# Pair sums of the second batch's input: adding transfers given out by GpSimd in place of GpSimd additions, in a Fourier transform with a feed-forward layer

## The chip, the cores and the metric

The kernel runs on one core of a Trainium2 chip. The metric is the device time of one execution in microseconds (us); three runs of the kernel before gave 1673.82, 1674.25 and 1674.61 us, so the median is 1674.25.

## The reference

```python
X = np.fft.fft(x, axis=1)                 # x: 8 x 3008 x 256, float32
X = np.fft.fft(X, axis=2)
x = X.real.astype(np.float32).reshape(24064, 256)
h = x @ w_in                              # 256 x 2048
g = np.where(h >= 1, h, np.where(h <= -1, 0.0, (h + 1) ** 2 / 4))
out = (g @ w_out).astype(np.float32)      # 2048 x 256
```

## The kernel before

**The work.** For each of the eight batches the kernel makes the transform in two stages of small matrix products (3008 = 64 x 47). Stage one (`stage1_sums`, product on L424) multiplies a folded input tile `x` by cosine and sine matrices into a PSUM bank called `s`, and ScalarE copies the bank to the tile `z` (`stage1_copies`, L458, four copies a tile). Stage two (L554) gives the tiles `pqh` and `pql`, high and low halves of a float32 number. From batch 1 on (`PLAIN = 1`) the input comes as seven tiles (`XT = 7`) that the host has laid out as four rows r of the same samples with signs of position and frequency turned; rows 0+1 and 2+3 are the *pair sums*, and their sum and difference are what stage one multiplies.

The feed-forward layer follows in *units*: 48 a batch, one for each of 16 blocks of 128 hidden features and each of three column chunks of 482 or 512 positions. `gemm1` (L599) makes two banks `uv` from `pqh`, `pql` and the halves `wh`, `wl` of w_in; VectorE makes `us` and `h` from them (L602, L605, L606), ScalarE the activation `a` (L611, L612), VectorE the gate in place in `h` (L629), ScalarE its high half `gh` (L632), and GpSimd the low half `gl` (`low_halves`, L652, two instructions, one for each of the two signs of position). `gemm2` (L728) adds three products to each of the four banks `acc`: `gh` by `woh`, `gh` by `wol`, `gl` by `woh`. Units 0 to 17 are an exception: they have no `gl`, since the native float32 product is used there.

**The first batch.** Until unit 23 the order of the work is written out by hand. START, AHEAD, AMID and STEPS are tables of steps by unit; a letter is a step, the number after it is its argument. There the weights, which are 64-bit floats, are turned into 32-bit ones by VectorE, ScalarE and GpSimd (`convert_*`, tiles `cv` and `raw`; `convert_scale` on GpSimd is L325), w_in is folded with the second transform by TensorE (`fold_w_in`, tile `wps`, L378), and the second batch's input is loaded (`L`, `load_x`, L163) and folded on GpSimd (`M`, `fold_next`): for tile 0 by two steps, for tiles 1 to 6 by four each: `fold_pair` twice (L186), `fold_sum` (L191), `fold_difference` (L197).

**What sets the order.** A scheduler puts every engine's instructions into one fixed sequence when the program is built; each engine then works through its own in order and waits at an instruction until what it needs is there. SyncE's queue gives out the transfers, also in order. Buffers are few: an `x` tile has four places (tag "xt"), and converting the weight piece 13 also uses one of them (`RAW[13]`), so that the load of x_2 into that place waits for VectorE's last step on piece 13 (L309), and the loads of x_5, x_4 and x_6 wait for stage one of x_0, x_1 and x_2. Stage one of most of these tiles uses a single bank ("fft"), which is free again when ScalarE has copied it.

Of the kernel before, what the change touches and what calls it, by code (L numbers as in the profile page):

```python
# [14 lines left out]
ALU = mybir.AluOpType  # L15
# [12 lines left out]
PLAIN = 1  # L28
# [18 lines left out]
def _constants():  # L47
# [36 lines left out]
)  # L84
AHEAD = {1: "p12 v2 G0 q11", 2: "b3", 3: "p13 d3", 5: "L1", 6: "u1 d4", 7: "e14", 8: "M R1", 11: "d6", 12: "e15 r2 a10 M e7", 14: "s4", 15: "M b10", 16: "M", 17: "u2 d10 Q2 M u3 B11", 19: "u4 s7 c15", 20: "Q4", 23: "d15", 27: "M", 29: "M", 32: "M"}
AMID = {0: "p11 b2", 1: "h E1 q12", 4: "q13", 5: "p14", 6: "q14 A9", 7: "f2 B9 a8", 8: "b9 c8", 9: "c6", 11: "M a7 f4", 12: "b7 e10", 14: "d13", 16: "O1", 17: "a15 e11 a14 f7", 18: "b11", 19: "u5 b14 O5", 20: "L5", 22: "u6", 23: "M", 24: "M", 28: "M M", 31: "M M", 32: "M"}
STEPS = {
    0: "c2 | D1",
    1: "L0 e5",
# [4 lines left out]
    6: "a12 d5",  # L94
    7: "b8 | b12 M s2 f3",
    8: "s3 d8 | a6 b6 e13",
    9: "r1 | c9 M",
    10: "u0 | d9 M L2",
    11: "f5 A13 R2",
    12: "s5 | c12 l11 B13 b13",  # L100
    13: "c13 d12 |",
    14: "f6 c7 d7",
    15: "M s6 Q0 |",
    16: "A11 c10 M |",
    17: "R3 | M",
    18: "O3 r3 c11 d11 M b15",
    19: "c14 d14",
    20: "L4 |",
    22: "L6 |",
    23: "u7",  # L110
    24: "M O6 | O7",
    25: "M |",
    26: "M |",
}
# [28 lines left out]
def fft_ffn_kernel(ctx: ExitStack, tc: tile.TileContext, x, xn, cst, w_in, w_out, out):  # L143
    nc = tc.nc
# [6 lines left out]
    xt, yt, zt, nyb, pq = {}, {}, {}, {}, {}  # L151
# [5 lines left out]
    def load_x(b, q):  # L157
        tag = "xt" if b or q < 4 else "gl"
        bufs = BUFS["xt"] if b or q < 4 else 4
        t = sb.tile([P, 2, CH], F32, tag=tag, name=f"x_{b}_{q}", bufs=bufs)  # L160
        if b >= PLAIN:
            t = t.rearrange("p (r u) n -> p (r u n)", u=1).rearrange("p (r n) -> p r n", r=4)[:, :, : CH // (2 if q else 4)]
            nc.sync.dma_start(t, xn[b - PLAIN, q, :, :, : t.shape[2]])  # L163
        else:
            nc.sync.dma_start(t, x[b, q])
        xt[b, q] = t

    def fold_x(b, q, engine=None):

        t = xt.pop((b, q))  # L170
        engine = engine or nc.gpsimd
        y = sb.tile([96, CH], F32, tag="y", name=f"y_{b}_{q}", bufs=1) if q == 0 else t[:96, 0]
        first = engine.tensor_tensor(y, t[:96, 0], t[:96, 1], op=ALU.add)
        yt[b, q] = y
        if q == 0:
            n = P if b else NA
            y = t[:96, 1, :n]
            ins = engine.tensor_tensor(y, t[:96, 0, :n], t[:96, 1, :n], op=ALU.subtract).ins
            tc.add_manual_dep(ins, first.ins.name, no_sync, reason="order of issue")
            yt[b, "d"] = y  # L180
        return first.ins

    def fold_pair(b, q, r):

        t = xt[b, q][: NT * NH]
        return nc.gpsimd.tensor_tensor(t[:, r], t[:, r], t[:, r + 1], op=ALU.add).ins  # L186

    def fold_sum(b, q):

        t = xt[b, q][: NT * NH]  # L190
        return nc.gpsimd.tensor_tensor(t[:, 1], t[:, 0], t[:, 2], op=ALU.add).ins  # L191
# [153 lines left out]
    def behind_vector(ins):  # L345
        last = [ins for ins in traced if ins.engine == mybir.EngineType.DVE][-1]
        tc.add_manual_dep(ins, last.name, data_sync, reason="beside VectorE's next steps")
# [130 lines left out]
    def fold_behind_activation(b, q):  # L478
        if q == 0:
            folding.extend([(b, q, fold_first_pairs), (b, q, fold_first_signs)])  # L480
            return
        folding.extend([(b, q, fold_pair, 0), (b, q, fold_pair, 2), (b, q, fold_sum), (b, q, fold_difference)])
# [6 lines left out]
    folding, ahead = [], []  # L489
    for q in range(XT):  # L490
        if q == 0:
            ahead += [(1, q, fold_first_pairs), (1, q, fold_first_signs)]
        else:
            ahead += [(1, q, fold_pair, 0), (1, q, fold_pair, 2), (1, q, fold_sum), (1, q, fold_difference)]

    def fold_next():
        if not ahead:
# [89 lines left out]
    def signs(i):  # L587
        return (slice(0, 1), slice(1, 2)) if i == n_units - 1 else (slice(0, 2),)

    def gemm1(i):  # L590
# [11 lines left out]
        nc.vector.scalar_tensor_tensor(us, nyb[b, k][:, :n], delta[:, f : f + 1], uv[0], op0=ALU.mult, op1=ALU.add)  # L602
        run_steps(AHEAD.get(i, ""))
        h = sb.tile([P, 2, CH], F32, tag="h", name=f"h_{i}", bufs=4)[:, :, :n]
# [3 lines left out]

        run_steps(AMID.get(i, ""))
        for sg in signs(i):  # L610
# [148 lines left out]
    def piece_sums(n):  # L759
# [10 lines left out]
        "m": lambda n: nc.sync.dma_start(cm, cst[:, _OFF[2] : _OFF[6]]),  # L770
        "h": lambda n: load_halves(),
        "x": lambda n: load_x(0, n),
        "y": lambda n: fold_x(0, n, nc.vector),
        "L": lambda n: load_x(1, n),
        "Y": lambda n: behind_vector(fold_x(1, n)),
        "g": lambda n: fold_x(0, n),
        "p": piece_sums,
# [29 lines left out]
    def run_steps(names):  # L807
        for s in names.split():
            steps[s[0]](int(s[1:] or 0))
# [17 lines left out]
    for i in range(n_units + LAG):  # L827
        if i < n_units:
            b, r = divmod(i, per)
            r0 = NEXT if b == 0 else 0  # L830
            if r == r0:
                pending = fft_pieces(b + 1) if b + 1 < NB else []
            if b + 2 < NB and r == LOADED[b + 2 >= PAIRED]:
                for q in range(4):
                    load_x(b + 2, q)
            gemm1(i)
            if b == 0 and units[i][2] == NFT - 2:
                load_parts(units[i][1])
# [117 lines left out]
```

## Time and profile before

| | us |
|---|---|
| median of three runs | 1674.25 |
| the profiled execution's own time | 1674.61 |
| its span, first to last instruction | 1672.4 |
| TensorE busy | 1667.3 |
| VectorE busy | 1393.8 |
| ScalarE busy | 1328.9 |
| GpSimd busy | 1189.6 |

The span is 2.2 us shorter than that execution's own time. An engine's busy time is the time in which at least one of its instructions ran. In the rows below, PE is TensorE, DVE VectorE, ACT ScalarE, POOL GpSimd, SPq the queue of SyncE. A name such as `cv` stands for all buffers of that name; L325 is line 325 of the kernel.

### The profile page before, as it was taken

How to read it: one execution, taken by the hardware profiler on the slowest of the kernel's cores; microseconds unless marked ns; L12 is line 12 of the kernel's file. 1: busy time of each engine (PE TensorE's matmuls, PEld its weight loads, DVE VectorE, ACT ScalarE, POOL GpSimd, SP SyncE). 2: the span in 40 equal slices, each digit the busy share in tenths (PEclk: the TensorE clock that was granted, in tenths of full speed). 3: DMA queues.
4: the chain of work that ended last, by engine and by line, in shares of the span. 5: the costliest groups of instructions: out<-in, count | busy, mean ns of one | idle time of the engine just before them, and what ended most of it. 6: DMA issues, size and time to landing. Idle time of an engine off the chain costs nothing.

```text
span 1672.4 us, 21444 instructions
## 1 busy us (share of the span) xinstructions
PE 1667.3 (100%) x7733; PEld 1384.9 (83%) x7733; DVE 1393.8 (83%) x1745; ACT 1328.9 (79%) x1529; POOL 1189.6 (71%) x960
## 2 busy tenths in 40 slices
PE   9999999999999999999999999999999999999999
PEld 6558888888888888888888888888888888888887
DVE  8999899878888887888878788787887877788777
ACT  6778878877888778887787877878778888777786
POOL 2458878767787677877779677796777855666664
PEclk9999999999999999999999999999999999999999
DMA  9113111110012000120010200201001010000000
GB/s 351 49 51 123 52 51 64 43 39 33 25 45 74 7 26 29 42 75 7 26 67 4 75 7 26 69 12 64 14 19 63 1 37 32 1 26 23 2 25 26
DMA packets 35705, 75.49 MB, mean 45 GB/s; under 512 B 4624, under 2 KB 13840, under 8 KB 35600
## 3 DMA queue, kind: packets, MB, share of 16 engines
q1 hardware_dynamic: 35420, 74.00, 12.4%
q8 instruction: 60, 0.98, 0.2%
q14 instruction: 45, 0.37, 0.1%
q10 hardware_dynamic: 180, 0.14, 0.0%
HBM read 46.31 MB, written 27.81 MB: 44 GB/s over the span
## 4 chain that ended last, share of the span: by engine, by line
PE 99%; DVE 1%; issue 0%; POOL 0%; DVEq 0%; POOLq 0%
PE acc L728 62%; PE uv L599 30%; PE s L424 2%; PE s L554 2%; PE wps L378 1%; PE warm_bank L752 0%; PE s L429 0%; PE acc L678 0%; DVE us L602 0%; DVE h L605 0%; DVE h L606 0%; PE ny L528 0%; DVE g L625 0%; DVE pql L243 0%; PE delta L357 0%
## 5 line engine op out<-in xcount | busy, mean ns | idle before, releaser
L652 POOL TENSOR_TENSOR gl<-h,gh 128x512 fp32r<-128x512 f32 (+1 forms) x728 | 917.7, 1283 | 383.1 <-PE acc L728 186.3
L611 ACT ACTIVATE a<-h,biases 128x1024 f32<-128x1024 f32 (+1 forms) x385 | 436.3, 1134 | 218.7 <-DVE h L606 216.5
L728 PE MATMUL acc<-gh,woh 128*128 128x512 f32 (+1 forms) x1456 | 563.1, 387 | 0.0
L728 PE MATMUL acc<-gh,wol 128*128 128x512 f32 (+1 forms) x1456 | 558.0, 383 | 0.0
L728 PE MATMUL acc<-gl,woh 128*128 128x512 f32 (+1 forms) x1456 | 557.8, 383 | 0.0
L629 DVE SCALAR_TENSOR_TENSOR h<-a,h 128x1024 f32<-128x1024 f32 (+2 forms) x367 | 522.5, 1424 | 2.0 <-ACT a L612 1.1
L602 DVE SCALAR_TENSOR_TENSOR us<-nyb,delta,uv 128x512 f32<-128x512 f32 (+1 forms) x384 | 282.6, 736 | 205.3 <-PE uv L599 203.3
L632 ACT ACTIVATE gh<-h 128x1024 fp32r<-128x1024 f32 (+2 forms) x367 | 382.8, 1043 | 83.0 <-DVE h L629 62.7
L612 ACT ACTIVATE a<-a 128x1024 f32<-128x1024 f32 (+1 forms) x385 | 395.2, 1027 | 1.0
L728 PEld LDWEIGHTS acc<-gl,woh 128*128 128x128 f32 x1456 | 272.7, 187 | 51.6
L728 PEld LDWEIGHTS acc<-gh,woh 128*128 128x128 f32 x1456 | 272.9, 187 | 49.4
L728 PEld LDWEIGHTS acc<-gh,wol 128*128 128x128 f32 x1456 | 272.8, 187 | 49.0
L605 DVE TENSOR_TENSOR h<-us,uv 128x512 f32<-128x512 f32 (+1 forms) x384 | 260.1, 677 | 52.6 <-POOL gl L652 2.1
L599 PE MATMUL uv<-pqh,wh 128*128 128x512 f32 (+1 forms) x768 | 302.4, 394 | 0.0
L599 PE MATMUL uv<-pql,wh 128*128 128x512 f32 (+1 forms) x768 | 294.3, 383 | 0.0
L599 PE MATMUL uv<-pqh,wl 128*128 128x512 f32 (+1 forms) x768 | 294.2, 383 | 0.0
L606 DVE TENSOR_TENSOR h<-us,uv 128x512 f32<-128x512 f32 (+1 forms) x384 | 257.4, 670 | 0.0
L599 PEld LDWEIGHTS uv<-pqh,wh 128*128 128x128 f32 x768 | 143.9, 187 | 30.8 <-issue 3.8
L599 PEld LDWEIGHTS uv<-pqh,wl 128*128 128x128 f32 x768 | 143.8, 187 | 30.6 <-issue 4.5
L599 PEld LDWEIGHTS uv<-pql,wh 128*128 128x128 f32 x768 | 143.8, 187 | 27.5 <-DVE pql L243 0.4
L186 POOL TENSOR_TENSOR x<-x 120x256 f32<-120x256 f32 x84 | 99.2, 1182 | 14.7 <-DVE h L629 5.3
L458 ACT ACTIVATE z<-s 64x240 f32<-64x240 f32 (+1 forms) x196 | 69.0, 352 | 4.4 <-PE s L424 1.8
(100 smaller groups left out, 786.4 us busy)
## 6 DMA issues: line engine op xcount, KB each, us to landing
x<-in_xn_dram SPq DMA_DIRECT2D x42, 512.0 KB, 3.7
out_dram<-o SPq DMA_DIRECT2D x26, 512.0 KB, 2.8
out_dram<-o SPq DMA_DIRECT2D x14, 482.0 KB, 2.8
nyb<-nyr SPq DMA_DIRECT2D x24, 256.0 KB, 3.2
x<-in_x_dram SPq DMA_DIRECT2D x8, 512.0 KB, 7.1
raw<-in_moe_w_in_dram SPq DMA_DIRECT2D x4, 512.0 KB
raw<-in_moe_w_out_dram SPq DMA_DIRECT2D x4, 512.0 KB, 8.9
part<-o SPq DMA_DIRECT2D x4, 512.0 KB
```

The source lines that it names most:

```text
L186: return nc.gpsimd.tensor_tensor(t[:, r], t[:, r], t[:, r + 1], op=ALU.add).ins
L458: nc.scalar.activation(z[to, :, at : at + n], src[:, :, t0 : t0 + n], AF.Copy)
L599: nc.tensor.matmul(t[:, :n], w[m][:, cols], r[:, m], start=(j == 0), stop=(j == 2))
L602: nc.vector.scalar_tensor_tensor(us, nyb[b, k][:, :n], delta[:, f : f + 1], uv[0], op0=ALU.mult, op1=ALU.add)
L605: nc.vector.tensor_tensor(h[:, 0], us, uv[1], op=ALU.subtract)
L606: last_h = nc.vector.tensor_tensor(h[:, 1], us, uv[1], op=ALU.add).ins
L611: nc.scalar.activation(a[:, sg], h[:, sg], AF.Relu, bias=half, scale=0.5)
L612: nc.scalar.activation(a[:, sg], a[:, sg], AF.Square)
L629: g = nc.vector.scalar_tensor_tensor(h[:, sg], a[:, sg], 1.0, h[:, sg], op0=ALU.min, op1=ALU.max).ins
L632: nc.scalar.activation(gh[:, sg], h[:, sg], AF.Copy)
L652: ins = nc.gpsimd.tensor_tensor(gl[:, sg], h[:, sg], gh[:, sg].bitcast(F32), op=ALU.subtract).ins
L728: nc.tensor.matmul(acc[:, :n], w, g[:, sg], start=(begin and j == 0), stop=(last and j == len(terms) - 1))
```

## The change

Rows 1 and 3 of tiles 1 to 6 of batch 1 are no longer loaded by SyncE. SyncE loads rows 0 and 2 alone (256 KB in place of 512 KB), and GpSimd gives out a second transfer, the step `K`, that reads rows 1 and 3 from HBM and adds them to the tile in SBUF. The twelve additions L186 of these tiles go, with the twelve steps `M` that placed them; `fold_sum` and `fold_difference` stay. Tile 0, and all later batches, are as before. K1 stands at unit 7, K3 at 8, K2 at 12, K4 at 22, K5 at 23, K6 at 24; the load L1 is at unit 5, L3 at 4, L2 at 10, L4 and L5 at 20, L6 at 22.

```diff
-    9: "r1 | c9 M",
+    9: "r1 | c9",
...
-            nc.sync.dma_start(t, xn[b - PLAIN, q, :, :, : t.shape[2]])
+            src = xn[b - PLAIN, q, :, :, : t.shape[2]]
+            if b == 1 and q:
+                nc.sync.dma_start(t[:, 0::2], src[:, 0::2])
+            else:
+                nc.sync.dma_start(t, src)
...
+    def add_pairs(q):
+
+        t = xt[1, q]
+        nc.gpsimd.dma_start(t[:, 0::2], xn[1 - PLAIN, q, :, 1::2, : t.shape[2]], accum_op=ALU.add)
...
-            ahead += [(1, q, fold_pair, 0), (1, q, fold_pair, 2), (1, q, fold_sum), (1, q, fold_difference)]
+            ahead += [(1, q, fold_sum), (1, q, fold_difference)]
...
+        "K": add_pairs,
```

Up to unit 24 TensorE, VectorE and ScalarE have the same sequence as before. Three places of the new program follow. In them `x_1_2` is tile 2 of batch 1, and the last number of a name only counts. Ten lines were added, so the changed kernel's L195 is the new transfer, L334 is the former L325, L661 the former L652, L200 and L206 the former L191 and L197, L433 the former L424, L608 and L737 the former L599 and L728.

**GpSimd around unit 12.** Before:

```order
L197 TENSOR_TENSOR x_1_1_458<-x_1_1_458 120x256
L325 TENSOR_TENSOR cv_12_522<-cv_12_522 128x512
L325 TENSOR_TENSOR cv_13_702<-cv_13_702 128x512
L316 TENSOR_TENSOR cv_7_687<-cv_7_687,raw_wol_153 128x512
L325 TENSOR_TENSOR wo_1_680<-cv_7_687 128x512
L186 TENSOR_TENSOR x_1_2_668<-x_1_2_668 120x256 x2
```

After:

```order
L206 TENSOR_TENSOR x_1_1_458<-x_1_1_458 120x256
L195 DMA x_1_2_668<-in_xn_dram 128x2x256
L334 TENSOR_TENSOR cv_12_522<-cv_12_522 128x512
L334 TENSOR_TENSOR cv_13_702<-cv_13_702 128x512
L325 TENSOR_TENSOR cv_7_687<-cv_7_687,raw_wol_153 128x512
L334 TENSOR_TENSOR wo_1_680<-cv_7_687 128x512
```

The two additions of x_1_2 stood behind the scaling of the weight pieces 12 and 13; the transfer that takes their place stands ahead of it.

**GpSimd from unit 20 on, after the change** (before, `gl_20` followed on `gl_19` at once, and the pair additions of tiles 4 to 6 stood behind `gl_23`, `gl_24`, `gl_25` and `gl_28`):

```order
L661 TENSOR_TENSOR gl_19_1043<-h_19_968,gh_19_1008 128x482 x2
L195 DMA x_1_4_1011<-in_xn_dram 128x2x256
L661 TENSOR_TENSOR gl_20_1085<-h_20_1000,gh_20_1036 128x482 x2
L334 TENSOR_TENSOR wo_3_987<-cv_15_898 128x512
L206 TENSOR_TENSOR x_1_3_445<-x_1_3_445 120x256
L195 DMA x_1_5_1004<-in_xn_dram 128x2x256
L661 TENSOR_TENSOR gl_21_1123<-h_21_1030,gh_21_1068 128x482 x2
L195 DMA x_1_6_1071<-in_xn_dram 128x2x256
L661 TENSOR_TENSOR gl_22_1158<-h_22_1057,gh_22_1107 128x482 x2
L200 TENSOR_TENSOR x_1_4_1011<-x_1_4_1011 120x256
```

The transfers of tiles 4, 5 and 6 now stand ahead of `gl_20`, `gl_21` and `gl_22`.

**TensorE at the same place, after the change** (before, each unit's `gl` products stood among its `gh` products, and the products of x_1_1, x_1_2 and x_1_3 were apart by a whole unit or two):

```order
L433 MATMUL s1_1_1_1193<-halves_340,x_1_1_458 128x120 x4
L608 MATMUL uv_26_0_1217<-pqh_0_1_297,wh0_68 128x512
L608 MATMUL uv_26_0_1217<-pqh_0_1_297,wl0_70 128x512
L608 MATMUL uv_26_0_1217<-pql_0_1_298,wh0_68 128x512
L433 MATMUL s1_1_2_1237<-halves_340,x_1_2_668 128x120 x4
L433 MATMUL s1_1_3_1321<-halves_340,x_1_3_445 128x120 x2
L737 MATMUL acc_12_0_870<-gl_20_1085,woh_498 128x482
L737 MATMUL acc_12_2_872<-gl_20_1085,woh_498 128x482
L737 MATMUL acc_12_1_871<-gl_20_1085,woh_498 128x482
L737 MATMUL acc_12_3_873<-gl_20_1085,woh_498 128x482
```

Ahead of these rows now stand the products of x_1_0 (two), the eight `gh` products of unit 20 and the six of `uv_25`; behind them come seven `gh` products of unit 21, its `gl` products in the same split manner, the other three of `uv_26`, and unit 22. The scheduler has moved the four `gl_20` products behind the stage-one products of three tiles.

## Rows read from the trace of the kernel before

**Rows 1.** The page: engines' busy time, and the chain that ended last.

```profile
PE 1667.3 (100%) x7733; PEld 1384.9 (83%) x7733; DVE 1393.8 (83%) x1745; ACT 1328.9 (79%) x1529; POOL 1189.6 (71%) x960
...
PE 99%; DVE 1%; issue 0%; POOL 0%; DVEq 0%; POOLq 0%
```

**Rows 2.** TensorE's waits for others, whole span: us in total, times, longest.

```profile
PE warm_bank L752 <- POOL warm L747: 1.3, 1, 1.3
```

**Rows 3.** Stretches: length, busy us (instructions) of each engine, clock, DMA share, GB/s.

```profile
0.00:40.00 40.00, 38.52 (x186) 26.28 (x187) 32.28 (x63) 24.27 (x47) 10.10 (x11) 1.00 0.96 363
40.00:140.00 100.00, 100.00 (x326) 60.14 (x325) 97.44 (x142) 77.66 (x102) 52.67 (x48) 1.00 0.13 48
140.00:180.00 40.00, 40.00 (x200) 34.14 (x199) 36.76 (x41) 35.85 (x50) 38.06 (x31) 1.00 0.41 138
180.00:1660.00 1480.00, 1480.00 (x6985) 1257.15 (x6984) 1221.11 (x1493) 1188.89 (x1330) 1087.72 (x872) 1.00 0.10 34
```

**Rows 4.** L186 among tile x's instructions, first 260 us: ns min/median/max, first and last start.

```profile
L186 POOL TENSOR_TENSOR x<-x x18: 726/742/1727, 72.9 to 256.7; 120x256 f32<-120x256 f32 x18
```

**Rows 5.** The same view: SyncE's issues of the loads of x from batch 1 on.

```profile
L163 SPq DMA_DIRECT2D x<-in_xn_dram x13: 327/338/1055, 31.1 to 259.5; - x13
```

**Rows 6.** Order of time, SyncE, 88 to 95 us (start, length), and its queue's waits, 60 to 100 us.

```profile
90.76 0.33 SPq L163 DMA_DIRECT2D x<-in_xn_dram  x1
91.19 2.41 SPq L367 DMA_DIRECT2D delta<-row  x4
...
SPq L163 <- DVE cv L309: 10.7, 1, 10.7
```

**Rows 7.** DMA issues, 137 to 160 us: KB each, median us from issue to landing.

```profile
x<-in_xn_dram SPq DMA_DIRECT2D x1, 256.0 KB, 3.0
```

**Rows 8.** Order of time, GpSimd, 81 to 97 us.

```profile
82.12 0.73 POOL L197 TENSOR_TENSOR x<-x 120x256 f32<-120x256 f32 x1 [3.16 <-DVE cv L281]
86.25 1.40 POOL L325 TENSOR_TENSOR cv<-cv 128x512 f32<-128x512 f32 x1 [3.39 <-DVE cv L309]
90.88 1.27 POOL L325 TENSOR_TENSOR cv<-cv 128x512 f32<-128x512 f32 x1 [3.23 <-DVE cv L309]
```

**Rows 9.** Order of time, TensorE, 89 to 97 us.

```profile
92.70 1.88 PE L378 MATMUL wps<-cv,cm 128*128 128x512 f32 x4
94.02 0.79 PE L599 MATMUL uv<-pqh,wh 128*128 128x482 f32 x1
```

**Rows 10.** Order of time, TensorE, 118 to 205 us.

```profile
137.09 0.60 PE L424 MATMUL s<-halves,x 120*128 120x120 f32 x4
137.45 0.46 PE L728 MATMUL acc<-gh,woh 128*128 128x482 f32 x1
...
140.11 0.39 PE L599 MATMUL uv<-pqh,wh 128*128 128x512 f32 x1
...
141.47 1.05 PE L424 MATMUL s<-halves,x 120*128 120x120 f32 x8
142.28 0.46 PE L728 MATMUL acc<-gh,woh 128*128 128x482 f32 x1
```

**Rows 11.** SyncE's load into the place of x_1, tile x, 142 to 143 us.

```profile
L163 SPq DMA_DIRECT2D x<-in_xn_dram x1: 339/339/339, 142.6 to 142.6; - x1
```

**Rows 12.** Groups by shape, ScalarE, 120 to 190 us: busy us, mean ns, idle before.

```profile
L458 ACT ACTIVATE z<-s 64x240 f32<-64x240 f32 x24 | 8.9, 371 | 0.4
```

**Rows 13.** Order of time, GpSimd, 0 to 330 us.

```profile
130.16 2.42 POOL L652 TENSOR_TENSOR gl<-h,gh 128x482 fp32r<-128x482 f32 x2 [1.16 <-DVE h L629]
133.77 2.72 POOL L652 TENSOR_TENSOR gl<-h,gh 128x482 fp32r<-128x482 f32 x2 [1.19 <-DVE h L629]
136.43 2.23 POOL L325 TENSOR_TENSOR wo<-cv 128x512 f32<-128x512 f32 x1
138.63 0.74 POOL L197 TENSOR_TENSOR x<-x 120x256 f32<-120x256 f32 x1
139.32 3.32 POOL L652 TENSOR_TENSOR gl<-h,gh 128x482 fp32r<-128x482 f32 x2
```

More of the change, by code (lines that the diff above doesn't have):

```diff
@@ L84 @@
 )
-AHEAD = {1: "p12 v2 G0 q11", 2: "b3", 3: "p13 d3", 5: "L1", 6: "u1 d4", 7: "e14", 8: "M R1", 11: "d6", 12: "e15 r2 a10 M e7", 14: "s4", 15: "M b10", 16: "M", 17: "u2 d10 Q2 M u3 B11", 19: "u4 s7 c15", 20: "Q4", 23: "d15", 27: "M", 29: "M", 32: "M"}
-AMID = {0: "p11 b2", 1: "h E1 q12", 4: "q13", 5: "p14", 6: "q14 A9", 7: "f2 B9 a8", 8: "b9 c8", 9: "c6", 11: "M a7 f4", 12: "b7 e10", 14: "d13", 16: "O1", 17: "a15 e11 a14 f7", 18: "b11", 19: "u5 b14 O5", 20: "L5", 22: "u6", 23: "M", 24: "M", 28: "M M", 31: "M M", 32: "M"}
+AHEAD = {1: "p12 v2 G0 q11", 2: "b3", 3: "p13 d3", 5: "L1", 6: "u1 d4", 7: "e14 K1", 8: "M R1", 11: "d6", 12: "e15 r2 a10 M e7 K2", 14: "s4", 15: "b10", 16: "M", 17: "u2 d10 Q2 u3 B11", 19: "u4 s7 c15", 20: "Q4", 22: "K4", 23: "d15", 24: "K6", 29: "M", 32: "M"}
+AMID = {0: "p11 b2", 1: "h E1 q12", 4: "q13", 5: "p14", 6: "q14 A9", 7: "f2 B9 a8", 8: "b9 c8 K3", 9: "c6", 11: "M a7 f4", 12: "b7 e10", 14: "d13", 16: "O1", 17: "a15 e11 a14 f7", 18: "b11", 19: "u5 b14 O5", 20: "L5", 22: "u6", 23: "M K5", 28: "M", 32: "M"}
 STEPS = {
@@ L96 @@
     8: "s3 d8 | a6 b6 e13",
-    9: "r1 | c9 M",
-    10: "u0 | d9 M L2",
+    9: "r1 | c9",
+    10: "u0 | d9 L2",
     11: "f5 A13 R2",
@@ L102 @@
     14: "f6 c7 d7",
-    15: "M s6 Q0 |",
+    15: "s6 Q0 |",
     16: "A11 c10 M |",
-    17: "R3 | M",
+    17: "R3 |",
     18: "O3 r3 c11 d11 M b15",
@@ L110 @@
     23: "u7",
-    24: "M O6 | O7",
+    24: "O6 | O7",
     25: "M |",
```

## The prediction

> **What bounds the kernel now.** I read the page's first part, then its chain of waits: TensorE is busy 1667.3 of 1672.4 us, and 99% of the chain that ended last is TensorE [rows 1]. Next, who it waits for: in the whole span one wait of 1.3 us, for the zeros of the warm-up at the start [rows 2]. The stretches say the same for each stage: from 40 to 1660 us TensorE is busy in every microsecond, at a granted clock of 1.00 (2.4 GHz), while GpSimd is busy 53 of 100 us from 40 to 140 and 38 of 40 from 140 to 180 [rows 3]. So nothing that makes GpSimd lighter can be seen in the time: there is no wait for it to take away, and TensorE's own products stay the same ones. What the change can do is make TensorE wait, and every wait past 40 us is lost for good, since TensorE has no idle time later to give back. The question is therefore whether the six new transfers, at their places in GpSimd's sequence, hold up something TensorE needs.
>
> **What goes.** Twelve additions L186 of 0.73 to 1.73 us [rows 4], 9 to 21 us of GpSimd. Worth nothing by the rows above. The bytes from HBM are the same, and SyncE gives out as many transfers as before.
>
> **What comes: the price of giving out a transfer.** The trace has no transfer that GpSimd gives out. Call d the time for which one holds GpSimd, from the moment its wait is over. The nearest rows are SyncE's issues of these same loads: 0.33 us as a rule, 1.06 at the longest [rows 5]. No row says that GpSimd is quicker at it than SyncE, and an adding transfer has more to do than a load, so I take 1.06, the slow end, and keep 0.33 as the low bound. For the high bound I take a GpSimd instruction that is held up beside VectorE: the same addition takes 0.73 or 1.73 us [rows 4], so add 1.0: d = 2.06. In both cases the transfer itself lands beside other work, if the sum that reads it comes late enough: K1 and K3 are given out whole units ahead of their sums, while GpSimd is half idle [rows 3], and cost nothing; the sum of x_2 stands behind four weight steps of about 1.3 us and a fifth; the sum of x_4 comes 11 us behind K4, and those of x_5 and x_6 later still. If landing took twice the 3.0 us of a 256 KB load [rows 7], that cover would still do.
>
> **What moves, place A: K2.** It needs the load of x_2 landed. SyncE gives out that load at 90.76 only, after 10.7 us of waiting for VectorE's last step on weight piece 13, whose buffer it takes [rows 6]; that does not change. A 256 KB load lands 3.0 us after its issue [rows 7]: 93.76. Before, GpSimd scaled piece 12 at 86.25 and piece 13 at 90.88 [rows 8], and TensorE used them in the two `wps` products from 92.70 on [rows 9]. Now both scalings stand behind K2: 93.76 + 1.06 (d) + 1.40 = 96.22 for piece 12, + 1.27 = 97.49 for piece 13 (durations from [rows 8]). TensorE reaches `wps` at 92.70 as before and waits 3.52; the first product takes half of 1.88 us [rows 9], to 97.16, and the second waits 0.33. **A = 3.85 us**, and d comes into it once. Everything later is shifted by it; below I go on in the times of the trace of before.
>
> **Place B: K4, K5, K6, and TensorE's new order.** Prices: twelve `acc` products from 137.45 to 140.11, so 0.222 each; six `uv` products 1.36; the products of one stage-one tile 0.81 [rows 10]; ScalarE's four copies of its bank 4 x 0.371 = 1.48 [rows 12]; one `gl` instruction 1.21, half of 2.42 [rows 13].
>
> Step 1, the bank. TensorE passes the products of x_0 at 137.45, does eight `gh` products (to 139.22) and six `uv` (140.58), then x_1 (141.39) and three `uv` (142.07). x_2 needs the bank that ScalarE copies until 141.39 + 1.48 = 142.87: a wait of 0.80. Done at 143.68; x_3 needs the next copies, until 145.16: 1.48 more. Its two products end at 145.57. Before, a whole unit of products lay between these tiles and hid the copies.
>
> Step 2, `gl_20`. The load of x_4 takes the place of x_1; before, it was given out at 142.6 [rows 11], 1.13 after x_1's products began at 141.47 [rows 10]. Now these begin at 140.58, so the load goes out at 141.71 and lands at 144.71. K4 waits for it, and `gl_20` stands behind K4: 144.71 + 1.06 = 145.77, then 1.21 twice: 146.98 and 148.19. TensorE waits from 145.57 to 146.98 (1.41), does two products, and waits 0.77 for the second half. (Before, `gl_20` began at 133.77 [rows 13], 3.7 us ahead of unit 20's first `acc` product.)
>
> Step 3, `gl_21`. GpSimd goes on with the scaling of piece 15 (1.27), the difference of x_3 (0.74 [rows 13]), K5 (1.06) and `gl_21`: 152.47 and 153.68. TensorE, from 148.63, has seven `gh` products, to 150.18: it waits 2.29, then 0.77.
>
> Step 4, `gl_22`. K6 to 154.74, halves at 155.95 and 157.16. TensorE waits 0.47 and 0.54. From there the sums of x_4 and x_5 stand between the next `gl`, at 0.73 to 0.74 each, where four instructions stood before, and I count no more.
>
> **B = 0.80 + 1.48 + 1.41 + 0.77 + 2.29 + 0.77 + 0.47 + 0.54 = 8.5 us**; d comes in three times. VectorE stands still here too, since each `h` takes the buffer that a `gl` four units before has to have read; that is the same delay, not another.
>
> **The sum.** 3.85 + 8.5 = 12.4 us with GpSimd at its short durations. At those that the same instructions had in the trace of before (2.23 for the scaling, 2.72 and 3.32 for `gl_20` and `gl_21` [rows 13]) it is 0.96 + 0.30 + 0.90 = 2.2 more, 14.6. VectorE, beside which they were long, now stands still for part of the stretch, so I take the middle, 13.5. The profiled execution took 1674.61 us: 1688.1. Against the median, 0.36 lower, 1687.8. **Forecast: 1688 us**, 0.8% slower. A measurement of this kernel tells some 0.2%, 3.3 us, from no change. With d = 0.33 and the short durations the sum is 12.4 - 4 x 0.73 = 9.5 (1684); with d = 2.06 and the long ones 14.6 + 4.0 = 18.6 (1693).
>
> **Rivals.**
>
> *The queue is not held (not slower).* If a transfer's wait were kept beside GpSimd's sequence, so that what stands behind K2 and K4 runs on, A and the waits for `gl` vanish; only the bank waits of step 1 stay: 2.3 us, 1676.9, within 0.2%. It decides at K2: the scaling of piece 12 would start near 86 and not after 94. For it: no row shows GpSimd waiting for a transfer to be given out. Against it: SyncE's queue does wait in order; the transfers of `delta` stand behind the load of x_2 and go out right after it, at 91.19 [rows 6]. The Trainium skill (DMA: Bandwidth & Descriptors, Anatomy of one DMA — SWDGE (gpsimd) path) says that DMA engines never wait on semaphores and that any such wait happens on the issuing sequencer; by that rule this rival falls, and SyncE's rows agree, while no run so far shows it for GpSimd. Chance 0.07.
>
> *Each issue is held beside VectorE (slower still).* If VectorE, busy 97 of 100 us up to 140 [rows 3], keeps GpSimd from its part in the transfer as it holds the additions, d is 2.06: 1693, up to 1697 where more instructions of place B are held by 1.0 each. For it: 0.73 against 1.73 in [rows 4]. Against: VectorE itself stands still in most of B. Chance 0.22. The Trainium skill (SBUF — State Buffer, A bandwidth-pool intuition that's wrong (but worth ruling out)) has a transfer of GpSimd at about 0.62 us alone and 3.1 beside a VectorE copy, which waits for its descriptors; if all four deciding issues were held by those 2.5 us, the estimate by that page would be 14.6 + 10 = 24.6 us, 1699; no run here shows such a transfer yet.
>
> *Less of it.* The loads of x_2 and x_4, half as large, land a microsecond earlier, and d is small: 6 to 8 us, 1681 to 1683. Chance 0.03.
>
> *A gain.* It would need TensorE to have lost time to GpSimd without a wait on record; [rows 2, 3] leave no room. Chance 0.03, a microsecond or a few.
>
> **How the numbers follow.** The forecast has 0.65, between 1684 and 1692; the held issue 0.22, the lesser loss 0.03, no change 0.07, a gain 0.03. Slower by over 0.2%: 0.65 + 0.22 + 0.03 = 0.90; within: 0.07; faster: 0.03. The range 1681 to 1697 takes in the bounds of d and both lengths of GpSimd's work, and leaves out the cases without change and the tail beyond 1697.
>
> **What the profile after would show.** TensorE's busy time about as before, the span longer. In its waits: `wps` for GpSimd's scaling, near 4 us at about 93; stage one (L433) for ScalarE's copies, about 2.3; `acc` for `gl`, about 6, all before 165 us. GpSimd idle from 83 to about 94, released by the load of x_2, and again ahead of K4. After 180 us every unit as long as before. Wrong would be: GpSimd scaling piece 12 before 93 (the queue is not held); waits of TensorE for x_5 or x_6 (adding transfers land slowly); a loss spread over the span and not in these two places.

## The result, and the profile after

The changed kernel took 1694.3 us (median of four runs, 1694.06 to 1694.79) against 1674.05 for the kernel before on the same chips (1673.82 to 1674.61): a ratio of 1.012, 95% interval 1.0108 to 1.0133, so 20.2 us slower. The forecast was 1688, the range 1681 to 1697.

The page of the changed kernel, its span, the engines' busy time and the chain that ended last, which answer to [rows 1]:

```profile
span 1692.3 us, 21449 instructions
...
PE 1675.4 (99%) x7733; PEld 1386.6 (82%) x7733; DVE 1395.2 (82%) x1745; ACT 1329.0 (79%) x1529; POOL 1180.7 (70%) x954
...
PE 94%; DVE 3%; POOL 1%; issue 1%; DMA 0%; SPq 0%; DVEq 0%; POOLq 0%
```

GpSimd is lighter by 8.9 us and six instructions, and the span is 19.9 us longer. Two things are to be seen in TensorE's figures. Its time without work is now 1692.3 - 1675.4 = 16.9 us, before it was 1672.4 - 1667.3 = 5.1: **11.8 us of new idle time**. And the same 7733 products are busy for 1675.4 us instead of 1667.3: **8.1 us in which TensorE works, but more slowly**. The prediction spoke only of the first.

TensorE's waits for others over the whole span (answering to [rows 2]; us in total, times, longest):

```profile
PE wps L387 <- POOL cv L334: 4.5, 1, 4.5
PE acc L737 <- POOL gl L661: 4.3, 7, 1.1
PE s L433 <- ACT z L467: 2.5, 2, 1.6
PE warm_bank L761 <- POOL warm L756: 1.3, 1, 1.3
```

The three new lines are the three that were forecast, and add up to 11.3 us. The stretches (length, busy us and instructions of PE, PEld, DVE, ACT and POOL, granted clock, DMA share, GB/s; answering to [rows 3]) say where:

```profile
40.00:90.00 50.00, 50.00 (x156) 28.32 (x155) 49.00 (x76) 39.40 (x53) 19.52 (x19) 1.00 0.18 52
90.00:100.00 10.00, 5.49 (x12) 2.10 (x10) 5.11 (x8) 3.09 (x3) 5.25 (x5) 0.74 0.44 105
100.00:140.00 40.00, 40.00 (x129) 24.43 (x128) 36.95 (x51) 29.99 (x38) 21.13 (x17) 0.98 0.07 27
140.00:180.00 40.00, 33.48 (x144) 25.62 (x143) 27.70 (x31) 23.89 (x37) 22.75 (x20) 0.91 0.43 117
180.00:1680.00 1500.00, 1499.67 (x7078) 1273.08 (x7077) 1238.23 (x1512) 1206.35 (x1352) 1101.97 (x884) 1.00 0.10 34
```

TensorE is idle for 4.5 us between 90 and 100, for 6.5 between 140 and 180, and for the 0.3 of a last wait at 185 us: the places A and B. In these two stretches, and at the start of the one between them (0.98), the granted clock is no longer 1.00.

GpSimd in order of time, at place A (81 to 103 us) and at place B (135 to 175 us; start, length, engine, instruction, in brackets the idle time before and what ended it):

```profile
94.67 1.12 POOL L195 DMA_DIRECT2D x<-in_xn_dram  x1 [11.48 <-DMA x<-in_xn_dram]
95.51 2.79 POOL L334 TENSOR_TENSOR cv<-cv 128x512 f32<-128x512 f32 x2
...
152.09 1.15 POOL L195 DMA_DIRECT2D x<-in_xn_dram  x1 [13.29 <-DMA x<-in_xn_dram]
152.95 2.71 POOL L661 TENSOR_TENSOR gl<-h,gh 128x482 fp32r<-128x482 f32 x2
...
157.74 1.09 POOL L195 DMA_DIRECT2D x<-in_xn_dram  x1 [0.17 <-ACT woh L345]
158.53 2.73 POOL L661 TENSOR_TENSOR gl<-h,gh 128x482 fp32r<-128x482 f32 x2
162.03 1.10 POOL L195 DMA_DIRECT2D x<-in_xn_dram  x1 [0.78 <-PE acc L737]
```

GpSimd stands still for 11.48 us ahead of K2 and for 13.29 ahead of K4, both times until SyncE's load of the tile has landed, and the scalings and the `gl` that stand behind come after. Before, the scaling of piece 12 began at 86.25 [rows 8]; now it begins at 95.51, for a product that TensorE wanted at 92.7 [rows 9].

### The profile page after: what moved, and what is told of

It is laid out like the page before. It is cut to its first block, busy times and chain, and to the rows that moved or that the text cites. A ratio compares the mean times of both kernels' runs of the same rounds, so it can differ in the third digit from the quotient of the medians.

```text
span 1692.3 us, 21449 instructions
## 1 busy us (share of the span) xinstructions
PE 1675.4 (99%) x7733; PEld 1386.6 (82%) x7733; DVE 1395.2 (82%) x1745; ACT 1329.0 (79%) x1529; POOL 1180.7 (70%) x954
## 4 chain that ended last, share of the span: by engine, by line
PE 94%; DVE 3%; POOL 1%; issue 1%; DMA 0%; SPq 0%; DVEq 0%; POOLq 0%
PE acc L737 59%; PE uv L608 29%; PE s L563 3%; PE s L433 2%; POOL gl L661 1%; DVE g L634 1%; PE wps L387 1%; DVE h L614 0%; PE s L438 0%; DVE us L611 0%; DVE h L615 0%; DVE cv L318 0%; DMA raw<-in_moe_w_in_dram 0%; PE acc L687 0%; DVE cv L317 0%
## 5 line engine op out<-in xcount | busy, mean ns | idle before, releaser
L661 POOL TENSOR_TENSOR gl<-h,gh 128x512 fp32r<-128x512 f32 (+1 forms) x728 | 915.5, 1281 | 388.9 <-PE acc L737 184.5
L737 PE MATMUL acc<-gh,woh 128*128 128x512 f32 (+1 forms) x1456 | 563.8, 387 | 0.0
L737 PE MATMUL acc<-gl,woh 128*128 128x512 f32 (+1 forms) x1456 | 559.4, 385 | 4.4 <-POOL gl L661 4.3
L737 PE MATMUL acc<-gh,wol 128*128 128x512 f32 (+1 forms) x1456 | 558.7, 384 | 0.0
L737 PEld LDWEIGHTS acc<-gl,woh 128*128 128x128 f32 x1456 | 272.8, 188 | 60.0 <-POOL gl L661 8.9
L737 PEld LDWEIGHTS acc<-gh,woh 128*128 128x128 f32 x1456 | 273.4, 188 | 49.3
L737 PEld LDWEIGHTS acc<-gh,wol 128*128 128x128 f32 x1456 | 273.2, 188 | 49.4
L608 PE MATMUL uv<-pqh,wh 128*128 128x512 f32 (+1 forms) x768 | 303.2, 395 | 0.0
L608 PE MATMUL uv<-pqh,wl 128*128 128x512 f32 (+1 forms) x768 | 294.5, 384 | 0.0
L608 PE MATMUL uv<-pql,wh 128*128 128x512 f32 (+1 forms) x768 | 294.4, 383 | 0.0
L608 PEld LDWEIGHTS uv<-pqh,wh 128*128 128x128 f32 x768 | 144.1, 188 | 31.1 <-issue 4.1
L608 PEld LDWEIGHTS uv<-pqh,wl 128*128 128x128 f32 x768 | 144.0, 187 | 30.9 <-issue 4.8
L608 PEld LDWEIGHTS uv<-pql,wh 128*128 128x128 f32 x768 | 144.0, 187 | 27.5 <-DVE pql L252 0.4
L190 POOL TENSOR_TENSOR x<-x 120x256 f32<-120x256 f32 x72 | 85.2, 1183 | 6.5 <-DVE h L638 5.3
```

Source lines behind the costliest of these rows:

```text
L608: nc.tensor.matmul(t[:, :n], w[m][:, cols], r[:, m], start=(j == 0), stop=(j == 2))
L661: ins = nc.gpsimd.tensor_tensor(gl[:, sg], h[:, sg], gh[:, sg].bitcast(F32), op=ALU.subtract).ins
L737: nc.tensor.matmul(acc[:, :n], w, g[:, sg], start=(begin and j == 0), stop=(last and j == len(terms) - 1))
```

## The experiments

The theory after this reading: K2 and K4 hold GpSimd's queue until a load has landed, TensorE waits for what stands behind them (and, at B, for banks in its new order), and on top of the waits it loses time to a lower clock and to slow restarts. The rivals: the time goes with the transfers themselves, wherever they stand (issue and addition beside the engines); or it goes at one place alone, the other being hidden. The kernel before ran beside these on the same chips at 1673.94 and 1673.95 us.

### K2 later

`K2` moved from unit 12 to the middle of unit 14, behind the two scalings.

```diff
-AHEAD 12: "e15 r2 a10 M e7 K2"
+AHEAD 12: "e15 r2 a10 M e7"
-AMID 14: "d13"
+AMID 14: "d13 K2"
```

> Only K2 is moved, behind the scalings of weight pieces 12 and 13; all six adding transfers stay. Theory (GpSimd's sequence is held at K2 until x_2's load has landed): place A goes with its half-clock stretch, 7.0 us of the 20.2; B stays: 1687.3 us. Rival (each adding transfer costs its own 3.4 us wherever it stands): 1694, as the change. Seen in the trace: no wait of TensorE for the wps products, GpSimd busy between 83 and 94 us.

Measured: 1688.11 us, ratio 1.008 (1.0065 to 1.0096). TensorE's waits, but for the warm-up's:

```profile
PE acc L737 <- POOL gl L661: 3.8, 6, 1.1
PE s L433 <- ACT z L467: 2.5, 2, 1.6
...
```

The wait for `wps` has gone, and 6.2 us with it; the waits of place B are there as before. So K2's place costs 6.2 us by this run, not the 3.85 of the prediction.

### K4, K5 and K6 later

The three behind the `gl` that they stood ahead of, as far as their sums allow, and the `M` that use them later too.

```diff
-AHEAD 22: "K4", 24: "K6", 29: "M"
+AHEAD 28: "K5", 30: "M"
-AMID 23: "M K5", 28: "M"
+AMID 23: "M", 26: "K4", 28: "M M", 29: "K6", 30: "M"
-STEPS 25: "M |", 26: "M |"
```

> K2 stays where the change puts it; K4, K5 and K6 stand four units later, where their loads have landed. Theory: place B goes, 12.7 us with its half-clock stretch, A stays with 7.0: 1681 us. Rival (price of each transfer): 1694.

Measured: 1681.53 us, 1.0042 (1.0029 to 1.0056). But for the warm-up's, TensorE's one wait is that of place A:

```profile
PE wps L385 <- POOL cv L332: 4.5, 1, 4.5
...
```

Place B is thus worth 1694.3 - 1681.5 = 12.8 us, where the prediction had 8.5.

### Both moves

> Both moves, all six adding transfers still there. Theory: nothing of TensorE waits for GpSimd any more, 1674 us, the time of the kernel before, within 0.2%; no gain either, since TensorE had no wait for GpSimd to lose. Rival (price of each transfer, or their traffic): 1694. Rival (a lighter GpSimd is worth something): under 1670.

Both edits above together: 1675.01 us (11 runs, 1674.68 to 1676.7), 1.0006 (0.9998 to 1.0015), the same as before. TensorE waits for nothing but its warm-up, as in [rows 2]:

```profile
PE warm_bank L759 <- POOL warm L754: 1.3, 1, 1.3
```

GpSimd around K2 in this kernel, in order of time:

```profile
91.45 1.27 POOL L332 TENSOR_TENSOR cv<-cv 128x512 f32<-128x512 f32 x1 [3.26 <-DVE cv L316]
94.64 1.12 POOL L193 DMA_DIRECT2D x<-in_xn_dram  x1 [1.92 <-DMA x<-in_xn_dram]
```

The transfer waits for the same load, goes out at the same moment as in the changed kernel, and lasts as long; only the scalings are already done. The medians are 1.07 us apart, and the interval takes in no difference at all; its upper end, 0.15%, is 2.5 us. So of the 20 us the six transfers themselves cost about 1, which is not clear of the noise, and they bring nothing: the rival that the loss goes with them falls. The places add up too: 6.5 us from this kernel to that with K2's early place alone, 13.1 to that with B alone.

### K4 alone later

`K4` to the middle of unit 26; K5 and K6 keep their steps, and so does K2. The scheduler leaves K5 ahead of `gl_21`, but puts K6 behind `gl_24`.

```diff
-AHEAD 22: "K4"
-AMID 28: "M"
+AMID 26: "K4", 28: "M M M"
-STEPS 25: "M |", 26: "M |"
```

> Only K4 is moved behind gl_23; the scheduler then puts K5 ahead of gl_21 and K6 behind gl_24, and TensorE's sequence is that of the kernel before again. Theory: B is K4's wait for the load of x_4 and the order that the scheduler made of it; K5 alone, whose load has landed, costs at most its own issue of 1.1 to 1.4 us plus a restart: 1681 to 1684 us (A's 7.0 stays). Rival (K5 and K6 each hold GpSimd for as much as K4): 1689 or more.

Measured: 1682.78 us, 1.0051 (1.0037 to 1.0064). The scheduler puts TensorE's products in the order of the kernel before again. TensorE's waits:

```profile
PE wps L385 <- POOL cv L332: 4.4, 1, 4.4
PE acc L735 <- POOL gl L659: 1.4, 2, 1.1
```

So some 11 of B's 12.8 us hang on the place of K4, with the order of TensorE that comes with it: 11.5 by the medians, and 1.25 are left for K5 ahead of `gl_21`. This split is rough: in the profiled executions the clock at A was back at 0.95 between 100 and 101 us here and still at 0.50 in the changed kernel, so that A was about 0.8 us shorter here (the `acc` products behind it begin at 101.63, and at 102.43 there), and up to that much belongs to K5 and not to K4.

### K2 where it was, its load earlier

Piece 13 is converted through another buffer, so that the load of x_2 no longer waits for it. Every engine's sequence stays that of the changed kernel.

```diff
-RAW = {..., 13: "xt", ...}
+RAW = {..., 13: "gh", ...}
```

> Every engine has exactly the sequence of the change, K2 included, ahead of the scalings; only weight piece 13 is loaded into another buffer, so that x_2's load no longer waits for its conversion. Theory (what costs time at place A is K2's wait for that load, not its place, its issue or its adding): the load goes out some 10 us earlier, K2 does not wait, A goes: 1688 us. Rival (a transfer of GpSimd's ahead of the scalings delays them by its own price): 1693 or more.

Measured: 1687.18 us, 1.0078 (1.0063 to 1.0093). GpSimd in order of time:

```profile
83.48 1.12 POOL L195 DMA_DIRECT2D x<-in_xn_dram  x1 [0.56 <-DMA x<-in_xn_dram]
86.33 1.39 POOL L334 TENSOR_TENSOR cv<-cv 128x512 f32<-128x512 f32 x1 [1.73 <-DVE cv L318]
```

K2 stands ahead of the scalings as in the changed kernel, but goes out at 83.48 and not at 94.67, and the scaling starts at 86.33 as before. Place A has gone, and 7.1 us with it. What cost the time there is the landing of the load, not the transfer ahead of the scaling. (It is 0.9 us quicker than K2 later. The profiled executions differ in place B: from 156 to 159 us the granted clock was 1.00 here and 0.50 there, where it fell a second time. Why it did is not shown.)

### The same transfers without adding

> The six transfers of GpSimd stay in place but load rows 1 and 3 over rows 0 and 2 without adding, so the pair sums are left out. Theory (waits in the sequence): same places, same waits, 1694 us within 1.5. Rival (adding makes the issue or the landing dear): several us less, the issues clearly under 1.1 us and the landing nearer to 3.0 us than to the 4.1 of the adding ones.

```diff
-        nc.gpsimd.dma_start(t[:, 0::2], xn[1 - PLAIN, q, :, 1::2, : t.shape[2]], accum_op=ALU.add)
+        nc.gpsimd.dma_start(t[:, 0::2], xn[1 - PLAIN, q, :, 1::2, : t.shape[2]])
```

Measured: 1692.13 us, 1.0108 (1.0093 to 1.0123), 2.2 us less than with the adding. The new transfer's line in the changed kernel (ns min/median/max of one issue, and us to landing):

```profile
L195 POOL DMA_DIRECT2D x<-in_xn_dram x6: 1088/1126/1279, 54.0 to 162.0; - x6
...
DMA to landing us min/median/max: 4.0/4.1/5.5
```

The same line without the adding:

```profile
L195 POOL DMA_DIRECT2D x<-in_xn_dram x6: 727/772/927, 54.5 to 161.2; - x6
...
DMA to landing us min/median/max: 3.0/3.2/4.9
```

An adding transfer's issue is 0.35 us longer, and it lands 0.9 later, as the rival had it; but the rival's several us did not come, and what the issue adds at four places is a small part of the 20 us. The time lies 0.4 us below what the theory allowed. Not all of the 2.2 us need be the adding: at A the clock fell later in this profiled execution (from 94 to 97 us it was granted 1.00, and 0.63 in the changed kernel). The queue waits just the same without it (GpSimd idle 11.42 us ahead of K2).

### Place A with the idle time filled

The kernel with K4, K5 and K6 later, and in TensorE's wait at A nineteen products that nobody reads, into the bank that the next true product starts afresh.

```diff
+        if n == 6 and h == 0:
+            for _ in range(19):
+                nc.tensor.matmul(folds[n], wh[0][:, :P], wh[0][:, :CH], start=True, stop=True)
```

> The kernel with K4 to K6 later (1681.5 us, place A alone) with 19 products of w_in's high half with itself, 4.3 us of them, put into the bank of wps ahead of its own products, where TensorE waits for GpSimd at place A; the true products then start the bank afresh. Theory (about a third of A is the half clock after the idle stretch): TensorE stays at the full clock and the time falls by 2.0 to 2.2 us, to 1679.4. Rival (the clock has another cause, or costs nothing beyond the wait): 1681.5 or, with products that delay the true ones, more.

Measured: 1679.58 us (six runs, 1679.39 to 1679.84), 1.0033 (1.002 to 1.0045), 1.95 us quicker than the same kernel without the nineteen products. The stretches at A without them (columns as above):

```profile
94.00:98.00 4.00, 0.64 (x1) 0.50 (x2) 1.33 (x2) 1.80 (x2) 3.12 (x3) 0.75 0.49 131
98.00:102.00 4.00, 4.00 (x7) 1.88 (x6) 0.00 (x0) 0.83 (x2) 3.01 (x3) 0.50 0.39 66
```

And with them:

```profile
94.00:98.00 4.00, 3.76 (x17) 2.58 (x15) 1.33 (x2) 1.81 (x2) 3.06 (x3) 1.00 0.52 126
98.00:102.00 4.00, 3.91 (x13) 2.19 (x12) 1.41 (x3) 1.88 (x3) 3.14 (x3) 1.00 0.43 71
```

GpSimd's work is alike in both; the granted clock stays at 1.00 (2.4 GHz) where it fell to 0.50 (1.2 GHz), and TensorE does 13 products in four microseconds instead of 7. So 1.95 of A's 6.5 us are the clock, lost after the wait was over.

## Why the prediction was right in direction and 6 us short

**What bounds the kernel** held. GpSimd lost 8.9 us of work and gave nothing back, and with both places mended the time is that of before within 1.1 us: 1675.01.

**The range** took the time in, but by luck in part: its upper end was room for a d of 2.06 us and for long GpSimd instructions, and d came out at 1.1 to 1.4. What filled that room are terms that the sum did not have, given below.

**d** was near. Taken at 1.06, bounds 0.33 and 2.06; the issue measured 1.126, and 1.279 at most. Counted as the prediction defined it, from the moment the wait is over, it was 1.4 at K2: the load of x_2 landed at 94.1, as forecast 3.0 us after its issue at 91.1, and the scaling behind K2 began at 95.51.

**The rivals.** *The queue is not held* fell by the 11.48 and 13.29 us of idle time in the rows of GpSimd above. The rule of the Trainium skill (DMA: Bandwidth & Descriptors, Anatomy of one DMA — SWDGE (gpsimd) path) that the issuing sequencer does the waiting agrees with both. *Each issue is held beside VectorE* gave 1693 to 1697, and the time that came lies there, but not for its reason: all six issues took 1.09 to 1.28 us, the first of them at 54.0 us, in a stretch where VectorE was busy 49 of 50 us. The Trainium skill's 3.1 us for a transfer of GpSimd beside a VectorE copy (SBUF — State Buffer, A bandwidth-pool intuition that's wrong (but worth ruling out)) does not appear in these six. No run here tests it for a copy: beside the issue at 54.0 us VectorE ran a weight step (L285) and a gate (L634). A time inside a rival's bounds is no evidence for the rival; the duration of its instruction is. *Less of it* and *a gain* did not come.

**Place A** was 3.85 us in the prediction and 6.2 to 7.1 by the runs (6.2 with K2 later, 6.5 between the two kernels with K4 to K6 later, 7.1 with the earlier load). The traces agree: the `acc` products ahead of it begin 0.2 us earlier than before (89.04 and 89.27), those behind it 6.7 later (102.43 and 95.72). Its wait was sized nearly right: the `wps` products start at 97.14 instead of 92.70, 4.44 us late, 0.6 above the forecast, of which 0.35 is the slower step from landing to scaling. What was left out came after it. TensorE in order of time, the first rows behind the wait:

```profile
97.14 3.78 PE L387 MATMUL wps<-cv,cm 128*128 128x512 f32 x4 [4.51 <-POOL cv L334]
99.94 1.39 PE L608 MATMUL uv<-pqh,wh 128*128 128x482 f32 x1
```

From the first `wps` product to the next `uv` there are 2.80 us, before 1.32 [rows 9]. The stretches of one microsecond show why:

```profile
96.00:97.00 1.00, 0.00 (x0) 0.00 (x0) 0.00 (x0) 0.00 (x0) 1.00 (x2) 0.50 0.79 279
98.00:99.00 1.00, 1.00 (x2) 0.29 (x1) 0.00 (x0) 0.00 (x0) 1.00 (x2) 0.50 1.10 177
102.00:103.00 1.00, 1.00 (x5) 0.70 (x4) 0.90 (x2) 0.84 (x2) 0.00 (x0) 1.00 0.00 0
```

The clock fell to 1.2 GHz in the idle time and was still there while TensorE worked again, until after 101 us. The step that failed is "everything later is shifted by it", which took the products behind a wait to be as long as ever; the run with the filled wait puts 1.95 us on that.

**Place B** was 8.5 us (with the longer GpSimd rows up to 10.7) and is 12.8 by the runs. TensorE there, in order of time:

```profile
147.32 1.05 PE L433 MATMUL s<-halves,x 120*128 120x120 f32 x8
...
149.96 1.15 PE L433 MATMUL s<-halves,x 120*128 120x120 f32 x8 [0.88 <-ACT z L467]
152.70 1.12 PE L433 MATMUL s<-halves,x 120*128 120x120 f32 x4 [1.59 <-ACT z L467]
154.54 2.34 PE L737 MATMUL acc<-gl,woh 128*128 128x482 f32 x4 [0.73 <-POOL gl L661]
156.68 0.60 PE L737 MATMUL acc<-gh,woh 128*128 128x482 f32 x1
157.08 0.61 PE L737 MATMUL acc<-gh,wol 128*128 128x482 f32 x1
...
160.14 0.70 PE L737 MATMUL acc<-gl,woh 128*128 128x482 f32 x2 [0.44 <-POOL gl L661]
161.31 0.48 PE L737 MATMUL acc<-gl,woh 128*128 128x482 f32 x1 [0.46 <-POOL gl L661]
161.63 0.37 PE L737 MATMUL acc<-gh,wol 128*128 128x482 f32 x1
161.84 0.37 PE L737 MATMUL acc<-gl,woh 128*128 128x482 f32 x1
...
164.44 0.49 PE L737 MATMUL acc<-gl,woh 128*128 128x482 f32 x1 [1.11 <-POOL gl L661]
...
170.86 0.48 PE L737 MATMUL acc<-gl,woh 128*128 128x482 f32 x1 [1.05 <-POOL gl L661]
```

By the forecast's steps:

- *Step 1, the bank*: waits of 0.88 and 1.59 us, forecast 0.80 and 1.48. Right.
- *Steps 2 to 4, `gl`*: the load of x_4 went out 1.13 us after x_1's products began (148.45 and 147.32), as forecast. The waits for `gl` on record are 4.3 us against a forecast of 6.25, and one of 1.05 stands at 170.86, behind `gl_22`, where I "count no more". By the rows they are shorter because TensorE came later to each: from 152.8 to 159.6 us it ran at 1.2 GHz. Its seven `gh` products stand 0.40 apart (156.68 to 157.08), where 0.222 was reckoned: seven times 0.18 is 1.3 us for these alone. The four products of `gl_20` take 2.14 us (154.54 to 156.68) where 0.89 was reckoned, some of it a stop; with these and x_3's, about 3, an estimate.
- *Each stop* costs more than its wait on record. The product after it is 0.48 long and not 0.37, and the next follows after 0.32 (161.31 to 161.63) instead of 0.21. And the last product before a stop, which otherwise runs 0.16 us into the next one, ends alone. At about ten stops that makes some 2.7 us, an estimate from these rows.

So 11.3 us of waits, about 5 of clock at both places and about 3 of stops make some 19 of the 19.9 by which the span grew. Clock and stops are also the 8.1 us by which TensorE's busy time grew. Of the rest, 0.4 us stands behind TensorE's last product: from its start to the end of the span there are 4.3 us (1687.95 to 1692.3), before 3.9 (1668.54 to 1672.4). Of these shares the clock at A and the two places as wholes are shown by runs; the split inside B is read from the rows alone, and no kernel tried its parts one by one.

**After 180 us** "every unit as long as before" held, but for the first six us: TensorE is busy 1499.67 of 1500 us, and the last wait for `gl` ends at 185.50, not "before 165 us". The `acc` product that begins there is 19.3 us behind its time of before (166.19), that of 179.65 only 18.5 (161.19). "TensorE's busy time about as before" was wrong by the 8.1 us.

## What to carry to other kernels

A transfer that is given out by an engine which also computes is an instruction of that engine's sequence: cost it at the moment when what it waits for is there, and list what stands behind it in that sequence. Here the six transfers cost about 1 us, not clear of the noise, behind the work that TensorE waits for, and 20 us ahead of it. Where a wait is put into an engine that was never idle, add to the wait what the engine loses after it: here 4.5 us of wait at A became 6.5, and 6.8 at B became 12.8.

## What was not expected of the hardware

- The clock fell to 0.50 in the wait of 4.5 us at A, and in place B at 152.8 us, after waits of 0.88 and 1.59 with eight products between them. Here are two microseconds of B:

```profile
150.00:151.00 1.00, 1.00 (x8) 0.92 (x8) 0.00 (x0) 0.00 (x0) 0.00 (x0) 1.00 0.79 271
153.00:154.00 1.00, 0.82 (x4) 0.54 (x3) 0.00 (x0) 0.00 (x0) 1.00 (x2) 0.50 0.97 344
```

- GpSimd's own instructions behind an adding transfer were longer than behind the same transfer without adding. There the two scalings behind K2 took 2.49 us, and the weight step after them 1.28:

```profile
95.98 2.49 POOL L334 TENSOR_TENSOR cv<-cv 128x512 f32<-128x512 f32 x2
98.42 1.28 POOL L325 TENSOR_TENSOR cv<-cv,raw_wol 128x512 f32<-128x512 f32 x1
```

In the changed kernel it was 2.79 and, in this row, 1.58:

```profile
97.95 1.58 POOL L325 TENSOR_TENSOR cv<-cv,raw_wol 128x512 f32<-128x512 f32 x1
```

That is 0.3 us for the two scalings together and 0.3 for the weight step, while the transfer was on its way. The two kernels with K2 at the same place and K4 later show the same 2.79 and 1.58. Why was not tried.
